# Reciprocal denominators broadcast as bf16 in 16 transfers a half, scaled on ScalarE and multiplied on VectorE; the sixth product ahead of the second in the down stage

## The chip, the cores and the metric

The kernel runs on one core of one Trainium2 chip. The core has TensorE (PE, matmuls into PSUM), VectorE (DVE), ScalarE (ACT), GpSimd (POOL) and SyncE (SP, which here only issues DMA transfers). Each engine works through its own list of instructions in order and waits on semaphores for the others; 16 DMA engines move data between memory and SBUF. The metric is the device time of one launch in microseconds (us), the median of several runs.

## What is computed

The input `x` has 2048 tokens of 1024 features. Layer norm, then linear attention with 32 heads of 32, then a gated feed-forward of width 3584 on the same normalised input, whose output gates the attention's:

```python
phi = lambda t: jnp.where(t > 0, t + 1, jnp.exp(t)) + 1e-6
pq, pk = phi(q), phi(k)
kv = jnp.einsum("bhsd,bhse->bhde", pk, v)
z = jnp.einsum("bhsd->bhd", pk)
num = jnp.einsum("bhqd,bhde->bhqe", pq, kv)
den = jnp.einsum("bhqd,bhd->bhq", pq, z)[..., None] + 1e-6
o = num / den
...
xn = _layernorm(x, axis=-1)
s = _A_ref(xn, A_wqkv, A_wo)                      # o @ wo
g = silu((silu(xn @ w_gate) * (xn @ w_up)) @ w_down)
return x + s * g
```

Inputs, weights and output are bf16. The place that the change touches is the division by `den`, one number for each token and head.

## The kernel before

**Stages.** The first 140 us or so normalise `x`, transpose it (fp16, features on the partitions, in the arenas X and P), project keys and values and sum up `kv` and `z` over all tokens. Then `kv`, divided by `z` and masked to the diagonal blocks of the heads, is multiplied with `wo` into one 1024 x 1024 matrix M: 16 single matmuls, `m_build(g, c)`, each copied by ACT out of PSUM and stored to `m_scratch` in memory. With M, attention's second part is one product: s = (phi(q) z / den) @ M.

After that two halves of 1024 tokens (`p` = 0, 1) follow, each in the same order: the pairs q0, g0, q1, g1, g2 ... g13, then four down blocks. A pair holds two products of 1024 tokens by 1024 by 256 columns, each through a seven-product scheme (class `Set`, steps numbered 1 to 7) that takes seven multiplications of half-size blocks in place of eight; a pair has 56 matmuls of 128 x 512. The scheme needs sums and differences of weight blocks (`wload`, DVE), of activation blocks, and of results in PSUM: step 1 copies a bank on ACT, step 5 is copied to SBUF by ACT, steps 6 and 7 add on DVE. The results of steps 2, 3, 4 and 7 are final and go on to an evacuation by ACT or DVE. `PAIRSEQ` is the order in which a pair's steps stand.

- A q pair computes q and phi(q) into a bf16 tile in the arena H (`pq_tile`, 52 to 68 KB), and collects `den` on TensorE.
- A g pair (`gu_pair`) computes gate and up for 256 of the 3584 columns and writes silu(gate) * up to H.
- A down block `c` (`d_set`) covers 256 output columns: one product D of the gated values with `w_down` and one product S of the divided phi(q) with M. Their steps stand in the string `seq`. Step 6 adds step 5's copy to a bank on DVE, into another bank; step 7 then goes on in the old bank, so D7 waits for D6's addition. Step 4 of D needs seven differences R10 - T2, made by DVE just ahead into a ring of two buffers (`t4_ring`).

**Division, before.** Both halves call `recip(p)` and `normalise(p)` behind pair g1. `recip` takes the reciprocals of `den` on DVE (L769, L772) and stores them in fp32 to `r_scratch` in memory, 128 KB. `normalise` goes over 16 tiles (two token blocks `j` by eight head groups `g`). For each tile four transfers bring the reciprocals of four heads, each row repeated over 32 partitions, into a slot of `rr_ring`, a ring of three; ACT scales the slot by `z` (L308); POOL multiplies phi(q) with it (L791), and a transfer of 128 KB stores the result to `q_scratch`. So that is 64 broadcasts and 16 stores a half. `pq_load` reads `q_scratch` back before the down blocks, into X, as the operand of S.

**What sets the order.** Nothing runs as it is written: every operation is recorded in a `Plan` with what it reads and writes, and a list scheduler with its own cost figures (for a transfer 0.08 us of SP plus its bytes in a serial queue) puts each engine's operations into a fixed order. Within an engine nothing overtakes. All transfers are issued by SP, in one order, and a transfer that waits for a buffer holds up the ones behind it. Matmuls are recorded by the helper at L195, transposes by that at L202, ACT's work at L308, DVE's two-input operations at L315, transfers at L318. Weights come through `wload`: raw weights in a ring of three places, their sums in another ring of three. The names in the profile: `ps` is a PSUM bank, `W` the weight arena, `TM` the arena of temporaries, `H`, `X` and `P` as above, `zc` holds `z`.

Of the kernel before, what the change touches and what calls it, by code (L numbers as in the profile page):

```python
# [205 lines left out]
def build_kernel(nc, A_x, A_wqkv, A_wo, B_w_gate, B_w_up, B_w_down, out, WINDOW=6, NWARM=14):  # L206
# [12 lines left out]
    with ExitStack() as es:  # L219
# [20 lines left out]
        def named(*key):  # L240
            return Region([key])
# [23 lines left out]
        r_scr = nc.dram_tensor("r_scratch", [2, 4, 32, 256], F32)  # L265
# [54 lines left out]
        class Ring:  # L320
# [3 lines left out]
            def take(self):  # L324
                k = self.k % self.n
                self.k += 1
                return Slot(self.a, self.off + k * self.size, self.size, k)

# [277 lines left out]
        class Set:  # L606
# [4 lines left out]
            def __init__(self, ops, evac):  # L611
                self.ops, self.evac = ops, evac
# [15 lines left out]
            def step(self, m):  # L628
# [19 lines left out]
                elif m == 7:  # L648
                    self.grp(7, self.b, False)
                    d = d_ring.take()  # L650
# [13 lines left out]
        class Places(Ring):  # L664
            def __init__(self, arena, offs, size):
                self.a, self.offs, self.size, self.k = arena, offs, size, 0

            def take(self):
                k = self.k % len(self.offs)
                self.k += 1  # L670
                return Slot(self.a, self.offs[k], self.size, k)

        raw_ring = Places(W, (0, 8 * KB, 16 * KB), 8 * KB)
        cmb_ring = Places(W, (44 * KB, 24 * KB, 32 * KB), 8 * KB)
# [24 lines left out]
        def xset(stat, w, xv, evac):  # L699
            def ops(m):  # L700
                ws, wr = stat(w, m)
                xa, xr = xv[XOF[m]]
                return 4, [([(ws[q], xa[:, q, :]) for q in range(4)], [wr, xr])]
            return Set(ops, evac)
# [32 lines left out]
        def pq_tile(g, j):  # L737
            o = PQ0 + (2 * g + j) * KB
            return H.at(o, KB, BF16), H.reg(o, KB)

        def q_pair(p, s, stat, at=()):
# [18 lines left out]
            run_pair(xset(stat, 0, XV[p], evac(0)), xset(stat, 1, XV[p], evac(1)), at)  # L760

        def recip(p):
# [4 lines left out]
            ea, ra = e.ap(F32, 0, KB), e.ap(F32, KB, KB)  # L767
# [6 lines left out]
            dma([rr], [named("rscr", p)], r_scr[p].rearrange("q h t -> (q h) t"), ra, dsem("rs"), 128 * KB)  # L774

        def normalise(p):

            for j in range(2):
                for g in range(NG):
                    src, sr = pq_tile(g, j)  # L780
                    dst = src.bitcast(FP16)
                    e = rr_ring.take()
                    first = None
                    for hl in range(4):
                        rows = r_scr[p, 2 * j:2 * j + 2, 4 * g + hl, :].partition_broadcast(32)
                        o0 = dma([named("rscr", p)], [e.r],
                                 TM.t[32 * hl:32 * hl + 32, e.off // 2:(e.off + e.size) // 2].bitcast(F32).rearrange(
                                     "p (q t) -> p q t", q=2), rows, dsem("rr%d_%d" % (e.k, hl)), 64 * KB, first)
                        first = first or o0
                    act([z_r, e.r], [e.r], e.ap(F32), e.ap(F32), ACT.Identity, "sb", scale=zc[:, g:g + 1])  # L790
                    pool([sr, e.r], [sr], lambda h, dst=dst, src=src, e=e: h.tensor_tensor(  # L791
                        dst, src, e.ap(F32), ALU.mult), 1.35)
                    dma([sr], [named("q", p, g, j)], q_scr[p, g // 4, j, :, (g % 4) * 512:(g % 4 + 1) * 512], dst,
                        dsem("pq%d" % (g % 4)), 128 * KB)
# [17 lines left out]
        def gu_pair(p, n, stat):  # L812
# [11 lines left out]
            run_pair(xset(stat, 0, XV[p], ev_g), xset(stat, 1, XV[p], ev_u))  # L824
# [7 lines left out]
        def pq_load(p):  # L832
            for j in range(2):
                for k in range(2):
                    v, vr = xblock(X, 2 * j + k)
                    dma([named("q", p, 4 * k + g, j) for g in range(4)], [vr], v, q_scr[p, k, j].rearrange(
# [5 lines left out]
        t4_ring = Ring(W, 40 * KB, 2 * KB, 2)  # L842
# [51 lines left out]
        def d_set(p, c, Sx, mstat, first):  # L894
# [61 lines left out]
            dset = Set(dops, keep(gv, ACT.Silu))  # L956
            sset = xset(mstat, 0, QV, keep(sv, ACT.Identity))
# [123 lines left out]
```

## Time and profile before

| | us |
|---|---|
| median of three runs | 814.59 (814.16 to 815.94) |
| the profiled execution's own time | 815.25 |
| its span | 813.5 |

Between the profiled execution's time and its span lie 1.75 us outside the profile. A table of stages, from the windows of the profile (busy microseconds of each engine in the stretch):

| from : to | what | length | PE | DVE | ACT | POOL | granted clock |
|---|---|---|---|---|---|---|---|
| 0 : 140 | layer norm, keys, values | 140.0 | 133.8 | 75.6 | 56.8 | 11.5 | 1.00 |
| 140 : 208 | q0, g0, q1, g1, M | 68.0 | 66.9 | 50.7 | 38.7 | 4.4 | 1.00 |
| 208 : 262 | pairs with the division, first half | 54.0 | 42.4 | 27.1 | 23.5 | 16.7 | 0.91 |
| 262 : 360 | the rest of the g pairs | 98.0 | 98.0 | 69.2 | 37.5 | 0.0 | 1.00 |
| 360 : 480 | down blocks, first half | 120.0 | 116.9 | 73.8 | 28.9 | 0.0 | 1.00 |
| 480 : 542 | q0, g0, q1, g1 | 62.0 | 61.8 | 46.0 | 33.1 | 3.8 | 1.00 |
| 542 : 588 | pairs with the division, second half | 46.0 | 37.4 | 32.2 | 21.2 | 17.5 | 0.96 |
| 588 : 690 | the rest of the g pairs | 102.0 | 100.1 | 72.9 | 38.7 | 0.0 | 1.00 |
| 690 : 813 | down blocks, second half | 123.0 | 115.9 | 64.6 | 28.1 | 0.0 | 1.00 |

How to read it: an engine loses nothing by being idle unless another waits for it, so the column of TensorE against the length shows where time goes, and the views of waits show for whom it waited. In a row of a view, `[2.32 <-ACT ps L308]` is the idle time just before the instruction and the work that ended last before it began. A row like "x28 | 17.8, 289 | 47.0 <-ACT ..." gives the count, the busy time and mean in ns of one, and the idle time before the group.

### The profile page before, as it was taken

The page shows a single profiled execution, that of the slowest core. Times are in us where ns is not written, and L with a number is a line of the kernel's source. Part 1 is how long each engine was busy: PE and PEld are TensorE (multiplying, and loading weights), DVE is VectorE, ACT ScalarE, POOL GpSimd, SP SyncE. Part 2 cuts the span into 40 slices and gives each one's busy share as a digit, 9 for nine tenths or more (in the row PEclk, how much of TensorE's full clock was granted, in tenths as well). Part 3 has the DMA queues.
Part 4 walks back from the last instruction along what each step waited for, and adds up shares of the span by engine and source line. Part 5 has one row for each costly group of instructions (what it writes and reads, how often), then busy time and mean ns, then how long its engine had stood idle before and what let it go on. Part 6 is the DMA issues. An engine that isn't in the chain of part 4 may idle for free.

```text
span 813.5 us, 9849 instructions
## 1 busy us (share of the span) xinstructions
PE 773.1 (95%) x3800; PEld 349.5 (43%) x3818; DVE 512.1 (63%) x913; ACT 306.4 (38%) x505; POOL 53.9 (7%) x65
## 2 busy tenths in 40 slices
PE   8999999999778999999999999988899999999997
PEld 3445554444323444444444444333344444444443
DVE  5587434767365668686464776786767767657353
ACT  3344443565443343422322234545443333232131
POOL 2020000000341000000000000034200000000000
PEclk9999999999998999999999999999999999999999
DMA  9921000135665332551623522257852341351510
GB/s 307 261 66 39 1 1 1 52 111 140 181 189 151 104 104 54 140 173 47 195 77 92 146 74 84 73 161 210 257 142 65 92 135 34 91 160 48 155 39 27
DMA packets 147888, 91.10 MB, mean 112 GB/s; under 512 B 5248, under 2 KB 144768, under 8 KB 147840
## 3 DMA queue, kind: packets, MB, share of 16 engines
q1 hardware_dynamic: 147840, 90.46, 39.1%
q8 instruction: 30, 0.49, 0.3%
q14 instruction: 18, 0.15, 0.1%
HBM read 79.69 MB, written 10.75 MB: 111 GB/s over the span
## 4 chain that ended last, share of the span: by engine, by line
PE 69%; DMA 11%; SPq 8%; DVE 6%; ACT 2%; issue 2%; POOL 1%; DVEq 0%
PE ps L195 68%; SPq L318 8%; DVE W L315 3%; DMA W<-m_scratch 3%; DMA W<-in_B_w_up_dram 2%; DMA TM<-r_scratch 2%; PE ps L202 1%; DMA H<-in_A_wqkv_dram 1%; DMA W<-in_B_w_down_dram 1%; DVE TM L315 1%; ACT TM L308 1%; POOL H L791 1%; DVE ps L315 1%; DMA W<-in_A_wqkv_dram 1%; DMA m_scratch<-H 0%
## 5 line engine op out<-in xcount | busy, mean ns | idle before, releaser
L195 PE MATMUL ps<-X,W 128*128 128x512 f16 x1504 | 354.9, 385 | 21.7 <-DVE ps L315 12.9
L308 ACT ACTIVATE TM<-ps 128x512 f32<-128x512 f32 (+2 forms) x300 | 176.3, 595 | 274.7 <-PE ps L195 274.3
L195 PEld LDWEIGHTS ps<-X,W 128*128 128x128 f16 (+1 forms) x1504 | 144.5, 99 | 203.0 <-DVE ps L315 17.8
L315 DVE TENSOR_TENSOR W<-W 128x1024 f16<-128x1024 bf16 (+3 forms) x224 | 143.1, 654 | 80.5 <-DMA W<-in_B_w_up_dram 36.5
L195 PE MATMUL ps<-H,W 128*128 128x512 f16 x672 | 150.7, 379 | 2.5 <-DVE ps L315 2.2
L195 PE MATMUL ps<-P,W 128*128 128x512 f16 x512 | 123.4, 380 | 1.3 <-ACT ps L308 1.3
L315 DVE TENSOR_TENSOR ps<-ps,TM 128x512 f32<-128x512 f32 x80 | 55.6, 694 | 76.4 <-PE ps L195 76.3
L195 PEld LDWEIGHTS ps<-H,W 128*128 128x128 f16 (+1 forms) x672 | 64.9, 98 | 80.4 <-DVE ps L315 3.2
L315 DVE TENSOR_TENSOR TM<-ps,TM 128x512 f32<-128x512 f32 (+1 forms) x112 | 67.7, 606 | 48.4 <-PE ps L195 44.4
L308 ACT ACTIVATE ps<-ps 128x512 f32<-128x512 f32 x80 | 46.7, 584 | 96.7 <-PE ps L195 96.4
L195 PEld LDWEIGHTS ps<-P,W 128*128 128x128 f16 (+1 forms) x512 | 49.2, 98 | 60.4 <-ACT ps L308 1.8
L791 POOL TENSOR_TENSOR H<-H,TM 128x512 f16<-128x512 bf16 x32 | 42.3, 1332 | 459.1 <-ACT TM L308 459.1
L308 ACT ACTIVATE TM<-TM 128x512 f16<-128x512 f32 x52 | 32.6, 626 | 78.2 <-DVE TM L315 78.1
L315 DVE TENSOR_TENSOR H<-ps,TM 128x512 f16<-128x512 f32 x84 | 57.0, 685 | 6.7 <-PE ps L195 5.4
L195 PE MATMUL ps<-H,X 128*128 128x512 bf16 x249 | 56.4, 379 | 3.0 <-ACT X L308 2.0
L195 PE MATMUL ps<-H,P 128*128 128x512 bf16 x248 | 56.1, 379 | 0.4
L485 DVE TENSOR_SCALAR TM<-TM 128x512 f16<-128x512 f16 x64 | 17.8, 289 | 47.0 <-ACT TM L308 46.3
L315 DVE TENSOR_TENSOR W<-H 128x1024 f16<-128x1024 f16 x56 | 38.2, 701 | 1.1 <-PE ps L195 0.3
L308 ACT ACTIVATE TM<-TM,zc 128x512 f32<-128x512 f32 x32 | 23.0, 720 | 39.8 <-DMA TM<-r_scratch 39.8
L195 PEld LDWEIGHTS ps<-H,X 128*128 128x128 f16 x256 | 24.4, 98 | 30.9 <-ACT X L308 2.1
L195 PEld LDWEIGHTS ps<-H,P 128*128 128x128 f16 x256 | 24.8, 98 | 28.3
L195 PE MATMUL ps<-W 128*128 128x512 f16 x112 | 31.2, 380 | 2.2 <-DVE W L315 1.9
(60 smaller groups left out, 317.9 us busy)
## 6 DMA issues: line engine op xcount, KB each, us to landing
W<-in_B_w_gate_dram SPq DMA_DIRECT2D x28, 512.0 KB, 4.1
W<-in_B_w_up_dram SPq DMA_DIRECT2D x28, 512.0 KB, 5.4
W<-in_B_w_down_dram SPq DMA_DIRECT2D x16, 896.0 KB, 6.9
TM<-r_scratch SPq DMA_DIRECT2D x128, 64.0 KB, 2.7
W<-in_A_x_dram SPq DMA_DIRECT2D x16, 256.0 KB, 3.3
H<-in_A_wqkv_dram SPq DMA_DIRECT2D x4, 1024.0 KB, 9.0
W<-in_A_wqkv_dram SPq DMA_DIRECT2D x8, 512.0 KB, 7.5
q_scratch<-H SPq DMA_DIRECT2D x32, 128.0 KB, 2.7
```

The lines of the kernel that those rows point to most:

```text
L195: last = h.matmul(o, l, r, start=st, stop=sp, skip_group_check=True)
L202: last = h.transpose(o, i, ident)
L308: return PL.op("act", reads, writes, lambda h: h.activation(o, i, func, **kw), nel(o) / 1200.0 + (0.055 if src == "ps" else 0.095))
L315: return dve(reads, writes, lambda h: h.tensor_tensor(o, a, b, op), nel(o), 1.92 if fast else 0.96)
L318: return PL.op("sp", reads, writes, lambda h: h.dma_start(o, i), 0.08, sem=s, nbytes=nbytes, cow=cow)
L485: dve([e.r], [b.r], lambda h: h.tensor_scalar(ba, ea, 1.0, EPS_PHI, ALU.min, ALU.add), 512, 2.6)
L791: pool([sr, e.r], [sr], lambda h, dst=dst, src=src, e=e: h.tensor_tensor(dst, src, e.ap(F32), ALU.mult), 1.35)
```

## The change

*Denominators.* `r_scratch` is bf16: `recip` gets one more ACT operation that writes the reciprocals as bf16, and the store has 64 KB. `normalise` first sends 16 broadcasts, eight for each token block `j` (four head positions by two token quarters); each fills 32 partitions with eight head groups of 256 tokens. They go to 16 KB of H of their own, 68 to 84 KB, which hold `wo` until the last `m_build` of the first half; so the `m_build` products come in groups of 8 and 8 behind g0 and g1 (before: 6, 6 and 4 behind g0, g1 and g2). Every ACT scaling of a block `j` depends on all eight of its transfers. ACT scales in bf16 in place, DVE multiplies (before POOL), and four stores of 512 KB replace 16 of 128 KB, with `pq_tile` laid out to suit.

*Down blocks.* `seq` has D6 ahead of D2. `t4_ring` gets a third buffer, the last of three of `d_ring`; the down blocks keep to the other two (`dd_ring`).

```diff
-        r_scr = nc.dram_tensor("r_scratch", [2, 4, 32, 256], F32)
+        r_scr = nc.dram_tensor("r_scratch", [2, 4, 32, 256], BF16)
...
         def pq_tile(g, j):
-            o = PQ0 + (2 * g + j) * KB
+            o = PQ0 + ((2 * (g // 4) + j) * 4 + g % 4) * KB
...
-            dma([rr], [named("rscr", p)], r_scr[p].rearrange("q h t -> (q h) t"), ra, dsem("rs"), 128 * KB)
+            act([rr], [er], rb, ra, ACT.Identity, "sb")
+            dma([er], [named("rscr", p)], r_scr[p].rearrange("q h t -> (q h) t"), rb, dsem("rs"), 64 * KB)
+
+        RB0 = 68 * KB
 
         def normalise(p):
 
             for j in range(2):
+                rb = H.at(RB0 + j * 8 * KB, 8 * KB).rearrange("p (g q t) -> p g q t", g=NG, q=2)
+                rbr = H.reg(RB0 + j * 8 * KB, 8 * KB)
+                first = None
+                for hl in range(4):
+                    rows = r_scr[p, 2 * j:2 * j + 2, :, :].rearrange("q (g h) t -> h g q t", h=4)[hl]
+                    for q in range(2):
+                        o0 = dma([named("rscr", p)], [rbr], rb[32 * hl:32 * hl + 32, :, q, :],
+                                 rows[:, q, :].partition_broadcast(32), dsem("rr%d_%d_%d" % (j, hl, q)), 128 * KB, first)
+                        first = first or o0
                 for g in range(NG):
                     src, sr = pq_tile(g, j)
                     dst = src.bitcast(FP16)
-                    e = rr_ring.take()
-                    first = None
-                    for hl in range(4):
-                        rows = r_scr[p, 2 * j:2 * j + 2, 4 * g + hl, :].partition_broadcast(32)
-                        o0 = dma([named("rscr", p)], [e.r],
-                                 TM.t[32 * hl:32 * hl + 32, e.off // 2:(e.off + e.size) // 2].bitcast(F32).rearrange(
-                                     "p (q t) -> p q t", q=2), rows, dsem("rr%d_%d" % (e.k, hl)), 64 * KB, first)
-                        first = first or o0
-                    act([z_r, e.r], [e.r], e.ap(F32), e.ap(F32), ACT.Identity, "sb", scale=zc[:, g:g + 1])
-                    pool([sr, e.r], [sr], lambda h, dst=dst, src=src, e=e: h.tensor_tensor(
-                        dst, src, e.ap(F32), ALU.mult), 1.35)
-                    dma([sr], [named("q", p, g, j)], q_scr[p, g // 4, j, :, (g % 4) * 512:(g % 4 + 1) * 512], dst,
-                        dsem("pq%d" % (g % 4)), 128 * KB)
+                    o = RB0 + j * 8 * KB + g * KB
+                    zr, zrr = H.at(o, KB), H.reg(o, KB)
+                    act([z_r, zrr], [zrr], zr, zr, ACT.Identity, "sb", scale=zc[:, g:g + 1])
+                    tt([sr, zrr], [sr], dst, src, zr, ALU.mult, True)
+            for j in range(2):
+                for k in range(2):
+                    o = PQ0 + (2 * k + j) * 4 * KB
+                    dma([H.reg(o, 4 * KB)], [named("q", p, k, j)], q_scr[p, k, j], H.at(o, 4 * KB, FP16),
+                        dsem("pq%d%d" % (k, j)), 512 * KB)
...
-        t4_ring = Ring(W, 40 * KB, 2 * KB, 2)
+        t4_ring = Places([(W, 40 * KB), (W, 42 * KB), (TM, 8 * KB)], 2 * KB)
+        dd_ring = Ring(TM, 4 * KB, 2 * KB, 2)
...
             if first:
-                seq = "D1 D5 D2 D6 D7 S1 S5 D3 S2 S6 D4 S7 S3 S4"
+                seq = "D1 D5 D6 D2 D7 S1 S5 D3 S2 S6 D4 S7 S3 S4"
             else:
-                seq = "S1 S5 S2 S6 D1 S7 S3 D5 S4 D2 D6 D7 D3 D4"
+                seq = "S1 S5 S2 S6 D1 S7 S3 D5 S4 D6 D2 D7 D3 D4"
...
-                if p == 0 and n < 3 and k == "g":
-                    for _ in range(6):
+                if p == 0 and n < 2 and k == "g":
+                    for _ in range(8):
                         if mb:
                             m_build(*mb.popleft())
```

`Places` is a ring whose buffers stand at listed places; `first` lets the transfers into one buffer go side by side.

**SP, the first half behind pair g1, before.** A row gives the line, the operation, destination and source, the size, and how many stand in a row.

```order
L318 DMA TM<-r_scratch 32x2x256 x12
L318 DMA m_scratch<-H 128x512 x3
L318 DMA TM<-r_scratch 32x2x256 x4
L318 DMA q_scratch<-H 128x512
L318 DMA m_scratch<-H 128x512
L318 DMA TM<-r_scratch 32x2x256 x4
L318 DMA q_scratch<-H 128x512
L318 DMA m_scratch<-H 128x512
L318 DMA TM<-r_scratch 32x2x256 x4
L318 DMA q_scratch<-H 128x512
L318 DMA W<-in_B_w_gate_dram 128x8x256
L318 DMA W<-in_B_w_up_dram 128x8x256
```

The same place of the change:

```order
L318 DMA m_scratch<-H 128x512 x4
L318 DMA r_scratch<-TM 128x256
L318 DMA m_scratch<-H 128x512 x2
L318 DMA H<-r_scratch 32x8x256 x16
L318 DMA TM<-in_A_x_dram 128x4x256
L318 DMA m_scratch<-H 128x512 x2
L318 DMA W<-in_B_w_gate_dram 128x8x256
L318 DMA W<-in_B_w_up_dram 128x8x256
L318 DMA q_scratch<-H 128x2048 x3
L318 DMA W<-in_B_w_gate_dram 128x8x256
L318 DMA W<-in_B_w_up_dram 128x8x256
L318 DMA q_scratch<-H 128x2048
```

All 16 broadcasts now stand in one run, the weight loads behind them rather than among them, and the four stores between weight loads.

**ACT, the first half, in the pairs behind g1, before.** `TM<-TM,zc` is a scaling by `z`, `ps<-ps` the copy of step 1, `TM<-ps` the copies and silus, `H<-ps` the copies of `m_build`.

```order
L308 ACTIVATE TM<-TM,zc 128x512
L308 ACTIVATE H<-ps 128x512 x2
L308 ACTIVATE TM<-TM,zc 128x512
L308 ACTIVATE H<-ps 128x512
L308 ACTIVATE ps<-ps 128x512
L308 ACTIVATE TM<-TM,zc 128x512
L308 ACTIVATE H<-ps 128x512
L308 ACTIVATE ps<-ps 128x512
L308 ACTIVATE TM<-ps 128x512 x3
L308 ACTIVATE TM<-TM,zc 128x512
L308 ACTIVATE TM<-ps 128x512
L308 ACTIVATE TM<-TM,zc 128x512
```

And of the change, where a scaling reads `H<-H,zc`:

```order
L308 ACTIVATE ps<-ps 128x512
L308 ACTIVATE H<-H,zc 128x512
L308 ACTIVATE TM<-ps 128x512
L308 ACTIVATE H<-H,zc 128x512
L308 ACTIVATE ps<-ps 128x512
L308 ACTIVATE H<-H,zc 128x512
L308 ACTIVATE TM<-ps 128x512 x2
L308 ACTIVATE H<-H,zc 128x512 x8
L308 ACTIVATE TM<-ps 128x512
L308 ACTIVATE H<-H,zc 128x512 x2
L308 ACTIVATE TM<-ps 128x512
L308 ACTIVATE H<-H,zc 128x512 x3
```

The scalings, before spread over several pairs, stand close together, eight of them in one run.

**TensorE, a down block behind the first one (c = 2 of the first half), before.** `ps<-X,W` are matmuls of S, `ps<-H,W` and `ps<-W` of D, `ident,TM` the transposes of a finished tile. The four `ps<-X,W` are S4.

```order
L195 MATMUL ps<-X,W 128x512 x8
L195 MATMUL ps<-H,W 128x512 x7
L195 MATMUL ps<-X,W 128x512 x4
L195 MATMUL ps<-H,W 128x512 x35
L202 MATMUL ps<-ident,TM 128x128 x4
L195 MATMUL ps<-H,W 128x512 x28
L195 MATMUL ps<-W 128x512 x4
```

And of the change:

```order
L195 MATMUL ps<-X,W 128x512 x8
L195 MATMUL ps<-H,W 128x512 x7
L195 MATMUL ps<-X,W 128x512 x4
L195 MATMUL ps<-H,W 128x512 x42
L202 MATMUL ps<-ident,TM 128x128 x4
L195 MATMUL ps<-H,W 128x512 x14
L195 MATMUL ps<-TM,W 128x512 x2
L195 MATMUL ps<-H,W 128x512 x7
```

Steps 2, 3, 5, 6 and 7 of D are 14 matmuls each. Before, the 35 behind S4 are the second half of D5, then D2, then D6; the 28 are D7 and D3. Now the 42 are the second half of D5, D6, D2 and the first half of D7, so D2's 14 stand between D6 and D7, and the first of D4's operands here comes from the new buffer in TM.

40 lines of the change are left out of this document (20 added, 20 removed).

## The prediction

> **What bounds the kernel now.** First I read the page's head: TensorE is the bound, and what it loses sits in a few slices.
>
> ```profile
> PE 773.1 (95%) x3800; PEld 349.5 (43%) x3818; DVE 512.1 (63%) x913; ACT 306.4 (38%) x505; POOL 53.9 (7%) x65
> PE   8999999999778999999999999988899999999997
> PEclk9999999999998999999999999999999999999999
> ```
>
> Slices 11 to 13 and 29 to 31 (20.3 us each) read 7 and 8; they lie where each half divides phi(q) by its denominators. Windows cut there, beside a clean stretch and the two down stages, read:
>
> ```profile
> 262.10:360.00 97.90, 97.90 (x454) 44.29 (x453) 69.18 (x109) 37.45 (x64) 0.00 (x0) 1.00 0.38 105
> 380.00:477.00 97.00, 93.89 (x467) 42.54 (x466) 57.83 (x108) 24.33 (x42) 0.00 (x0) 1.00 0.42 117
> 710.00:811.00 101.00, 95.87 (x478) 42.89 (x475) 52.35 (x104) 24.70 (x43) 0.00 (x0) 1.00 0.30 84
> 207.90:262.10 54.20, 42.60 (x168) 16.66 (x168) 27.20 (x40) 23.51 (x41) 16.68 (x13) 0.91 0.64 188
> 542.30:588.20 45.90, 37.10 (x161) 15.66 (x159) 32.44 (x41) 21.16 (x36) 17.54 (x13) 0.96 0.77 221
> ```
>
> The columns are start:end and length, busy time of PE, PEld, DVE, ACT, POOL, then the granted clock, DMA share and GB/s. The clean stretch never idles. Its pace: 93 matmuls between these two starts take 20.09 us, 0.216 us each, so one weight pair (56 matmuls) takes 12.1 us.
>
> ```profile
> 339.83 20.25 PE L195 MATMUL ps<-X,W 128*128 128x512 f16 x93
> 359.92 2.32 PE L195 MATMUL ps<-H,W 128*128 128x512 f16 x10
> ```
>
> Window 207.9 holds 167 matmuls (timeline count; the window says 168): 36.1 us of work, so **18.1 us are lost**. Window 542.3 holds 160: 34.6 us, **11.3 us lost**. Part is waiting, part a slower clock behind the waits:
>
> ```profile
> 214.41 7.90 PE L195 MATMUL ps<-X,W 128*128 128x512 f16 x28 [2.32 <-ACT ps L308]
> 232.34 6.22 PE L195 MATMUL ps<-X,W 128*128 128x512 f16 x28 [1.72 <-ACT ps L308]
> 241.62 14.16 PE L195 MATMUL ps<-X,W 128*128 128x512 f16 x56 [3.07 <-DVE ps L315]
> 257.73 1.04 PE L195 MATMUL ps<-X,W 128*128 128x512 f16 x4 [1.94 <-DVE ps L315]
> ...
> 559.31 3.38 PE L195 MATMUL ps<-X,W 128*128 128x512 f16 x8 [2.99 <-DVE ps L315]
> ```
>
> The same 28 matmuls take 7.90 us behind a wait of 2.32 us and 6.22 behind 1.72. Who makes ACT and DVE late? The waits in 190 to 262 and SP's timeline say:
>
> ```profile
> ACT TM L308 <- DMA TM<-r_scratch: 26.4, 16, 5.2
> DVE W L315 <- DMA W<-in_B_w_up_dram: 10.7, 4, 3.6
> ...
> 233.32 4.41 SPq L318 DMA_DIRECT2D TM<-r_scratch  x4
> 243.03 3.06 SPq L318 DMA_DIRECT2D TM<-r_scratch  x4
> 249.46 0.80 SPq L318 DMA_DIRECT2D W<-in_B_w_up_dram  x1
> ```
>
> SP works through 64 broadcasts and 16 stores one by one, each waiting for a buffer that ACT and POOL must free (ring of three). Weight loads queue behind; DVE stands at their arrival with TensorE's additions behind it, and ACT at each broadcast with TensorE's copies behind it.
>
> **The change part by part.**
>
> ```profile
> L791 POOL TENSOR_TENSOR H<-H,TM 128x512 f16<-128x512 bf16 x32 | 42.3, 1332 | 459.1 <-ACT TM L308 459.1
> L308 ACT ACTIVATE TM<-TM,zc 128x512 f32<-128x512 f32 x32 | 23.0, 720 | 39.8 <-DMA TM<-r_scratch 39.8
> L315 DVE TENSOR_TENSOR TM<-TM 128x512 f16<-128x512 f16 x32 | 13.5, 420 | 13.2 <-ACT TM L308 13.2
> L485 DVE TENSOR_SCALAR TM<-TM 128x512 f16<-128x512 f16 x64 | 17.8, 289 | 47.0 <-ACT TM L308 46.3
> W<-in_B_w_up_dram SPq DMA_DIRECT2D x28, 512.0 KB, 5.4
> TM<-r_scratch SPq DMA_DIRECT2D x128, 64.0 KB, 2.7
> q_scratch<-H SPq DMA_DIRECT2D x32, 128.0 KB, 2.7
> ```
>
> *Queue.* Per half, 64 broadcasts and 16 stores become 16 and 4. At 0.47 us an issue (12 in 5.50 us in a row below) that is 37.6 us of SP against 9.4. All 16 broadcasts now have their own place, so none waits for ACT. Weights for pair 5 stand behind the 16, pair 6 behind three stores.
>
> ```profile
> 192.08 0.34 SPq L318 DMA_DIRECT2D r_scratch<-TM  x1
> ...
> 529.59 1.81 DMA r_scratch<-TM
> ...
> 531.41 5.50 SPq L318 DMA_DIRECT2D TM<-r_scratch  x12
> ```
>
> *When the first half's burst lands.* Pair 2 ends on TensorE at 207.9 now; four `m_build` matmuls move ahead of it (0.9 us) and, below, cost 1 us: 209.8. The new bf16 copy stands on ACT behind three evacuations of pair 2, done about 202.4, so the store leaves ten microseconds later than its 192.08, with nothing on TensorE waiting. It lands 1.8 later (529.59 to 531.41 in the chain), and 16 issues run from 204.4 to 212. An eighth is 128 KB in 256 pieces; eight are 1 MB in 512-byte pieces, just like a gate and up load, whose second lands 5.4 us after its issue. So the first eight are down at about 211, between 208.2 + 1.7 and 208.2 + 7.3 (least and most of the old broadcasts, row below).
>
> ```profile
> DMA to landing us min/median/max: 1.7/2.7/7.3
> ```
>
> *ScalarE.* 16 scalings in both versions; bf16 is not in the trace, so 0.60 to 0.72 us, the PSUM-source and fp32 rows; I take 0.62 start to start. In the first half all 16 stand between pair 3's first copy and pair 4's: 9.9 us beside pair 3's own eight evacuations of 0.5, 13.9 us of work in a 12.1 us pair. Pair 4's first copy thus comes at 225.7, where TensorE's fourth step wants it at 224.5. With some slip of the landing I charge **2.0**. In the second half four scalings stand in pair 2's tail, twelve in pair 3 (11.4 in 12.1): **1.0**. Ends: 0 and 7 for each, the upper if the burst lands 4 us later and the clock drops too.
>
> *VectorE* takes over the multiplication: 16 per half at 0.42 (bounds 0.29, a one-input op, and 0.69, fp32), 6.7 us across pairs 2 to 4, where the clean window leaves it idle 28.7 of 97.9, 3.5 us a pair. POOL's 1.33 us operations go; no one else used it. Three multiplications stand ahead of pair 3's first PSUM addition: scaled by 214.5, while that addition is due at 215.0. Cost zero, with 0.8 us of cover; past it, one for one.
>
> *The `m_build` products*, 8 + 8 instead of 6 + 6 + 4. Each needs an evacuation:
>
> ```profile
> L308 ACT ACTIVATE H<-ps 128x512 f16<-128x512 f32 x16 | 8.7, 601 | 2.3 <-PE ps L195 2.3
> 174.20 1.90 PE L195 MATMUL ps<-X,W 128*128 128x512 f16 x8 [0.67 <-DVE ps L315]
> ```
>
> Two more lengthen the ACT chain behind that 0.67 us wait by about 1.0 while TensorE gains 0.43 of work; the same after pair 1. Charge **1.0** (0 to 2).
>
> *Down stage.* D6 now stands ahead of D2, so 14 matmuls (3.0 us) cover the addition that D7 waits for; a third place serves the 701 ns subtractions of D4.
>
> ```profile
> 435.14 1.56 DVE L315 TENSOR_TENSOR W<-W 128x512 f16<-128x512 f16 x4 [1.03 <-DMA W<-m_scratch]
> ...
> 437.70 6.22 PE L195 MATMUL ps<-H,W 128*128 128x512 f16 x28 [0.21 <-DVE ps L315]
> 445.32 0.60 PE L195 MATMUL ps<-W 128*128 128x512 f16 x2 [0.21 <-DVE W L315]
> 467.02 6.22 PE L195 MATMUL ps<-H,W 128*128 128x512 f16 x28 [0.57 <-DVE ps L315]
> 474.87 0.61 PE L195 MATMUL ps<-W 128*128 128x512 f16 x2 [0.78 <-DVE W L315]
> ...
> 675.56 1.04 PE L195 MATMUL ps<-X,W 128*128 128x512 f16 x4 [1.69 <-DVE TM L315]
> ...
> 797.60 6.22 PE L195 MATMUL ps<-H,W 128*128 128x512 f16 x28 [0.57 <-DVE ps L315]
> ```
>
> Block 3 waits for nothing else (0.57, twice): gone. Blocks 1 and 2 have the addition behind the arrival of m_scratch, issued when S4 ends in both versions, so it is late again; about half stays. I take 2.0 from D6 and 0.5 from D4, **2.5** together; bounds 0 and 5, about the idle of the two down windows (3.1 and 5.1) without the tail. A late down-weight load (1.69 us of idle at 675) is untouched.
>
> [...] The trace lost clock behind waits of 1.94 to 3.07 us: 0.91 and 0.96 granted in the two stages, 1.00 elsewhere. [...]
>
> **Rivals.**
> 1. *The wait only moves.* ACT and DVE serve in order, and their first scaling waits for eight transfers at once. For: one microsecond of slack; 13.9 us of ACT work in a 12.1 us pair. Against: the 5.4 us landing. Price if the eight land at the old 7.3 us: 4 more a half plus 1.5 of clock, 11 in all: 798.
> 2. *The clock loss isn't the waits'.* Of 29.4 us lost, waits in the timeline make 20.3; 9.1 are clock. If that stays: 796. Against: 6.22 beside 7.90 above.
> 3. *It doesn't relieve the DMA.* As many pieces move as before (16 x 256 = 64 x 64), and the share there was 0.64 and 0.77. If pieces, not issues, held up the weights, half the gain goes: 801. Against: the share is short of full, and SP's stops come with full rings.
> 4. *Slower.* The eight broadcasts read the same 4 KB again and again; if that serialises them, the first scaling stops ACT, copies and TensorE one for one. It decides once the landing takes 18 us rather than 3 (14 us a half cancel the 28 gained); at 25 us the time is 829. The old broadcasts never took over 7.3.
>
> **How the numbers follow.** 18.1 + 11.3 - 2.0 - 1.0 - 1.0 + 2.5 = 27.9 us off the profiled run (span 813.5, run 815.25, so 1.75 around it): 787.4. The median of three is 814.59, 0.66 lower: **787**. Chances: forecast (781 to 793) 0.68, rival 1 (793 to 804) 0.17, rival 2 0.05, rival 3 0.06, slower 0.04. Everything going well, with no charges and 5 from the down stage, gives 780; the upper end takes in rivals 1 and 2: 780 to 799. 0.2% (1.6 us) is about what a measurement here can tell from no change: faster 0.95, same 0.01, slower 0.04.
>
> **What would show it.** Right: TensorE at nearly 10 of 10 in pairs 2 to 6 of both halves, clock 1.00 there; 32 broadcasts, issued at about 0.47; no DVE wait for up weights there; POOL empty after the start; DVE some 13 us busier; no wait of 0.57 at block 3's D7. Wrong: waits of over 2 us by TensorE for ACT's copies at pairs 3 and 4 (rival 1), a clock under 1.00 without waits (2), weights landing later than 6 us (3), broadcasts landing after ten or more (4).

## The result, and the profile after

The changed kernel takes 789.71 us (789.6 to 791.02, three runs) against 814.59: 0.9696 of the time before (95% interval 0.9672 to 0.9719). The profiled execution took 789.71 with a span of 787.9, so 25.6 us of span are gone; the prediction had 27.9 gone and a time of 787. The page's head and TensorE's slices:

```profile
PE 763.0 (97%) x3818; PEld 347.7 (44%) x3818; DVE 513.2 (65%) x945; ACT 305.0 (39%) x507; POOL 11.5 (1%) x33
...
PE   8999999999999999999999999999999999999997
...
PEclk9999999999999999999999999999999999999999
```

The 7s and 8s of slices 11 to 13 and 29 to 31 are gone, the granted clock reads 9 in every slice (0.999 over the run), and POOL is down to the work at the start. Where in the program did the time go? Four landmarks of TensorE's timeline cut every kernel here in the same way: the first matmul behind keys and values, the first matmul of D in the first half, the first den matmul of the second half, the first matmul of D there. For the kernel before the first two are at 140.74 and 359.92, and the others are (start, length, instruction):

```profile
486.86 0.29 PE L195 MATMUL ps<-H,Zh 128*32 128x256 bf16 x2
...
690.24 12.25 PE L195 MATMUL ps<-H,W 128*128 128x512 f16 x56
```

For the changed kernel:

```profile
140.40 0.40 PE L195 MATMUL ps<-ones,ident 128*128 128x128 f16 x4 [0.29 <-DVE H L585]
...
345.54 13.93 PE L195 MATMUL ps<-H,W 128*128 128x512 f16 x63
...
470.33 0.29 PE L195 MATMUL ps<-H,Zh 128*32 128x256 bf16 x2
...
665.51 12.25 PE L195 MATMUL ps<-H,W 128*128 128x512 f16 x56
```

| us | before | after | gain | prediction |
|---|---|---|---|---|
| A: to D of the first half (first division) | 219.18 | 205.14 | 14.0 | 18.1 - 2.0 - 1.0 = 15.1 |
| B: down blocks and what runs beside them, first half | 126.94 | 124.79 | 2.2 | B and D: 2.5 |
| C: to D of the second half (second division) | 203.38 | 195.18 | 8.2 | 11.3 - 1.0 = 10.3 |
| D: down blocks, second half, to the end | 123.26 | 122.39 | 0.9 | |

The rest, 0.3 us, is ahead of the first landmark. What TensorE still waits for in the two divisions stands in its timeline:

```profile
215.74 3.63 PE L195 MATMUL ps<-X,W 128*128 128x512 f16 x16 [1.55 <-ACT ps L308]
219.96 6.28 PE L195 MATMUL ps<-X,W 128*128 128x512 f16 x28 [0.59 <-DVE ps L315]
227.25 118.45 PE L195 MATMUL ps<-X,W 128*128 128x512 f16 x548 [1.02 <-ACT ps L308]
...
531.88 1.90 PE L195 MATMUL ps<-P,W 128*128 128x512 f16 x8 [1.51 <-ACT ps L308]
...
554.01 1.04 PE L195 MATMUL ps<-X,W 128*128 128x512 f16 x4 [1.12 <-DVE TM L315]
```

Three waits of 3.16 us in the first half and two of 2.63 in the second, in place of the rows of 1.72 to 3.07 before. 28 matmuls behind the second wait take 6.28, near the 6.22 of the kernel before behind 1.72 us and not the 7.90 behind 2.32. SP's timeline and ACT's show how the burst runs:

```profile
201.69 2.27 SPq L318 DMA_DIRECT2D r_scratch<-TM  x1
...
205.61 7.88 SPq L318 DMA_DIRECT2D H<-r_scratch  x16
```

```profile
213.38 0.72 ACT L308 ACTIVATE H<-H,zc 128x512 bf16<-128x512 bf16 x1 [2.89 <-DMA H<-r_scratch]
...
215.10 0.58 ACT L308 ACTIVATE ps<-ps 128x512 f32<-128x512 f32 x1
...
217.18 5.00 ACT L308 ACTIVATE H<-H,zc 128x512 bf16<-128x512 bf16 x8
```

Sixteen issues at 0.49 us each, never stopped. ACT comes free at 210.5, stands 2.89 us at the landing of the first eight, and only then gets to pair 3's copies; the one at 215.10 ends TensorE's wait of 1.55. From 217.18 eight scalings run at 0.62 us from start to start.

### The profile page after: what moved, and what is told of

It is laid out like the page before. It is cut to its first block, busy times and chain, and to the rows that moved or that the text cites. A ratio compares the mean times of both kernels' runs of the same rounds, so it can differ in the third digit from the quotient of the medians.

```text
span 787.9 us, 9684 instructions
## 1 busy us (share of the span) xinstructions
PE 763.0 (97%) x3818; PEld 347.7 (44%) x3818; DVE 513.2 (65%) x945; ACT 305.0 (39%) x507; POOL 11.5 (1%) x33
## 4 chain that ended last, share of the span: by engine, by line
PE 81%; DMA 10%; ACT 4%; DVE 3%; SPq 2%; issue 1%; ACTq 0%
PE ps L195 79%; DMA W<-m_scratch 4%; ACT H L308 2%; PE ps L202 2%; SPq L318 2%; DMA H<-in_A_wqkv_dram 1%; DMA W<-in_B_w_down_dram 1%; DMA H<-r_scratch 1%; DVE W L315 1%; DMA W<-in_B_w_up_dram 1%; ACT TM L308 1%; DVE ps L315 1%; DMA m_scratch<-H 0%; DVE TM L315 0%; ACT ps L308 0%
## 5 line engine op out<-in xcount | busy, mean ns | idle before, releaser
L195 PE MATMUL ps<-X,W 128*128 128x512 f16 x1504 | 346.7, 379 | 7.7 <-DVE TM L315 2.8
L315 DVE TENSOR_TENSOR W<-W 128x1024 f16<-128x1024 bf16 (+3 forms) x224 | 137.3, 629 | 73.2 <-DMA W<-in_B_w_down_dram 34.3
L195 PE MATMUL ps<-H,W 128*128 128x512 f16 x672 | 153.3, 379 | 4.2 <-DVE ps L315 4.0
L308 ACT ACTIVATE TM<-TM 128x512 f16<-128x512 f32 (+1 forms) x54 | 33.5, 620 | 56.6 <-DVE TM L315 56.4
L315 DVE TENSOR_TENSOR H<-H 128x1024 f16<-128x1024 f16 (+1 forms) x74 | 41.6, 571 | 12.2 <-ACT H L308 11.2
L315 DVE TENSOR_TENSOR W<-H 128x1024 f16<-128x1024 f16 x38 | 25.4, 685 | 0.5
L308 ACT ACTIVATE H<-H,zc 128x512 bf16<-128x512 bf16 x32 | 20.8, 716 | 5.0 <-DMA H<-r_scratch 5.0
L495 DVE SCALAR_TENSOR_TENSOR W<-ps,TM 128x512 bf16<-128x512 f32 x32 | 22.0, 688 | 0.8
```

The costliest lines, as they stand in the source:

```text
L195: last = h.matmul(o, l, r, start=st, stop=sp, skip_group_check=True)
L308: return PL.op("act", reads, writes, lambda h: h.activation(o, i, func, **kw), nel(o) / 1200.0 + (0.055 if src == "ps" else 0.095))
L315: return dve(reads, writes, lambda h: h.tensor_tensor(o, a, b, op), nel(o), 1.92 if fast else 0.96)
L495: dve([src_r, b.r], [out_r], lambda h: h.scalar_tensor_tensor(out_ap, src, 0.0, ba, ALU.max, ALU.add), 512)
```

## The experiments

Each edit is to the changed kernel unless it says otherwise. The kernels before and after ran again beside them on other chips, where the kernel before took 816 to 817 us, so times are compared as ratios to it and the stages by the landmarks above. The division's code is the same in five profiles (the changed kernel twice and the three of the down blocks): A and C together are 399.2 to 400.5 us there, so a difference of 1.3 there is within the spread of single profiles.

| us | A | B | C | D | A + C | B + D | ratio to before (95%) |
|---|---|---|---|---|---|---|---|
| before | 219.18 | 126.94 | 203.38 | 123.26 | 422.6 | 250.2 | 1 |
| changed | 205.14 | 124.79 | 195.18 | 122.39 | 400.3 | 247.2 | 0.9696 (0.9672 to 0.9719) |
| after_again | 205.41 | 124.97 | 194.41 | 121.94 | 399.8 | 246.9 | 0.9676 (0.9646 to 0.9705) |
| e4_pool_mult | 214.05 | 124.37 | 197.30 | 121.03 | 411.4 | 245.4 | 0.9767 (0.9727 to 0.9808) |
| e5_before_dve_mult | 216.80 | 128.40 | 204.89 | 124.38 | 421.7 | 252.8 | 0.9989 (0.9966 to 1.0012) |
| e6_64_transfers | 223.66 | 125.73 | 217.17 | 123.67 | 440.8 | 249.4 | 1.0191 (1.0151 to 1.0231) |
| e7_first_eight_twice | 207.30 | 124.51 | 197.81 | 121.80 | 405.1 | 246.3 | 0.9734 (0.9710 to 0.9758) |
| e8_no_scaling | 208.24 | 123.39 | 195.39 | 122.22 | 403.6 | 245.6 | 0.9705 (0.9670 to 0.9740) |
| e10_no_scaling_late | 201.89 | 123.34 | 191.80 | 121.75 | 393.7 | 245.1 | 0.9571 (0.9542 to 0.9600) |
| e13_scaling_late | 202.33 | 124.01 | 192.37 | 121.70 | 394.7 | 245.7 | 0.9585 (0.9559 to 0.9611) |
| e12_both | 201.51 | 122.50 | 190.26 | 119.02 | 391.8 | 241.5 | 0.9502 (0.9467 to 0.9538) |
| e1_division_only | 204.91 | 128.09 | 195.38 | 123.52 | 400.3 | 251.6 | 0.9706 (0.9670 to 0.9742) |
| e2_d6_only | 205.39 | 127.27 | 195.07 | 123.52 | 400.5 | 250.8 | 0.9696 (0.9666 to 0.9725) |
| e3_t4_only | 204.96 | 126.55 | 194.21 | 122.34 | 399.2 | 248.9 | 0.9681 (0.9658 to 0.9705) |

### Is it the transfers or the multiplication that moved?

The multiplications back on POOL:

```diff
-                    tt([sr, zrr], [sr], dst, src, zr, ALU.mult, True)
+                    pool([sr, zrr], [sr], lambda h, dst=dst, src=src, zr=zr: h.tensor_tensor(
+                        dst, src, zr, ALU.mult), 1.35)
```

> The changed kernel with the multiplications back on POOL (1.33 us each, 21 us a half). Theory (the queue on SP and the waits tile by tile were what was lost): nothing on TensorE waits for the products before the down blocks, so only VectorE's slower operations beside POOL cost something, 0 to 3 us: 790 to 793. Rival (the slow multiplication on POOL held the old ring, and moving it is the gain): half or more of the 25 us comes back, 802 or more.

Neither: the span is 797.0, 9.1 over the changed kernel, and A and C take 11.0 more. TensorE has one long wait:

```profile
237.03 102.36 PE L195 MATMUL ps<-X,W 128*128 128x512 f16 x460 [5.78 <-DVE ps L315]
```

VectorE is late there because its own operations are slow: from 223.28 it works without a pause up to the addition that ends this wait. Its groups by form in 213 to 236, the stretch in which POOL multiplies almost without a pause, first for this kernel:

```profile
L315 DVE TENSOR_TENSOR H<-H 128x1024 f16<-128x1024 f16 x3 | 4.6, 1520 | 0.1
L315 DVE TENSOR_TENSOR W<-W 128x1024 f16<-128x1024 bf16 x3 | 4.5, 1538 | 2.9 <-DMA W<-in_B_w_up_dram 2.8
L315 DVE TENSOR_TENSOR H<-ps,TM 128x512 f16<-128x512 f32 x3 | 2.0, 683 | 1.5 <-ACT TM L308 1.5
```

and for the changed kernel:

```profile
L315 DVE TENSOR_TENSOR H<-ps,TM 128x512 f16<-128x512 f32 x4 | 2.7, 684 | 0.0
L315 DVE TENSOR_TENSOR W<-W 128x1024 f16<-128x1024 bf16 x4 | 2.7, 684 | 0.0
L315 DVE TENSOR_TENSOR H<-H 128x1024 f16<-128x1024 f16 x3 | 2.1, 684 | 0.0
```

Beside POOL these two-input operations with both operands in SBUF take 1520 and 1538 ns instead of 684; the three forms with an operand in PSUM stay at 683, 690 and 700 (684, 686 and 693 in the changed kernel). With two more of 1036 and 1037 ns, eight operations take 5.8 us more than without POOL, as long as TensorE's wait. The two sources differ only in where the multiplication runs, so POOL's work is what slows them. Moving the multiplication thus frees VectorE; the sum had POOL's operations as used by no one else, and counted nothing for it.

The move alone, made to the kernel before:

```diff
-                    pool([sr, e.r], [sr], lambda h, dst=dst, src=src, e=e: h.tensor_tensor(
-                        dst, src, e.ap(F32), ALU.mult), 1.35)
+                    tt([sr, e.r], [sr], dst, src, e.ap(F32), ALU.mult)
```

> The kernel before with one edit: VectorE multiplies (fp32 by bf16, about 0.69 us) in place of POOL; 64 broadcasts and 16 stores a half and the ring of three stay. Theory of the queue: SP still issues 80 transfers one by one and stops at the ring; at most a third of the gain, 806 to 815, or slower than before if VectorE now stands at ACT's scalings. Rival (POOL's 1.33 us sets when a slot of the ring is free): two thirds of the gain or more, 798 or less.

Nothing is gained (0.9989, interval across 1). The waits in 190 to 262 (us in total, times, longest) are those of before with VectorE in POOL's place:

```profile
ACT TM L308 <- DMA TM<-r_scratch: 23.5, 15, 5.8
...
DVE H L315 <- ACT TM L308: 9.4, 10, 2.4
DVE W L315 <- DMA W<-in_B_w_up_dram: 8.6, 4, 2.6
```

So POOL's 1.33 us did not hold the ring: ACT waits for the broadcasts nearly as long (23.5 us, before 26.4), and VectorE now stands 9.4 us at ACT's scalings. The multiplication's place is worth nothing with the old transfers and 11 us with the new ones.

### The number of transfers

The same bytes and the same pieces in 64 transfers, with a place for each tile:

```diff
-                for hl in range(4):
-                    rows = r_scr[p, 2 * j:2 * j + 2, :, :].rearrange("q (g h) t -> h g q t", h=4)[hl]
-                    for q in range(2):
-                        o0 = dma([named("rscr", p)], [rbr], rb[32 * hl:32 * hl + 32, :, q, :],
...
+                for g in range(NG):
+                    first = None
+                    for hl in range(4):
+                        rows = r_scr[p, 2 * j:2 * j + 2, 4 * g + hl, :].partition_broadcast(32)
+                        o0 = dma([named("rscr", p)], [H.reg(RB0 + j * 8 * KB + g * KB, KB)],
+                                 rb[32 * hl:32 * hl + 32, g, :, :], rows, dsem("rr%d_%d_%d" % (j, g, hl)), 32 * KB, first)
+                        first = first or o0
```

> The changed kernel with the broadcasts cut as before into 64 a half (four for each tile, 32 KB), each tile's scaling waiting for its own four, but with a place for every tile, so no ring. The bytes and the number of 512-byte pieces are those of the changed kernel; SP issues for 30 us rather than 8, with the weights of pairs 5 and 6 behind them. Theory (the issue count on the one queue is what was lost, as the prediction's term for the queue has it): the weights come late and VectorE stands at them, half or more of the gain goes, 800 to 808. Rival (it was the ring of three and the stops at it; issues alone are cheap): 788 to 794.

Worse than the theory, and slower than the kernel before: A and C take 440.8, 40 us more than with 16 transfers and 18 more than with the ring. SP issues for 30 us without a stop, a tile's four take 1.9 us, and ACT stands at every tile with TensorE's copy behind it; first SP, then ACT, then TensorE:

```profile
206.83 30.33 SPq L318 DMA_DIRECT2D H<-r_scratch  x64
238.14 0.50 SPq L318 DMA_DIRECT2D W<-in_B_w_gate_dram  x1
```

```profile
214.24 0.72 ACT L308 ACTIVATE H<-H,zc 128x512 bf16<-128x512 bf16 x1 [1.17 <-DMA H<-r_scratch]
216.19 0.72 ACT L308 ACTIVATE H<-H,zc 128x512 bf16<-128x512 bf16 x1 [1.23 <-DMA H<-r_scratch]
218.31 0.72 ACT L308 ACTIVATE H<-H,zc 128x512 bf16<-128x512 bf16 x1 [1.39 <-DMA H<-r_scratch]
218.93 0.58 ACT L308 ACTIVATE ps<-ps 128x512 f32<-128x512 f32 x1
```

```profile
219.57 8.34 PE L195 MATMUL ps<-X,W 128*128 128x512 f16 x28 [6.30 <-ACT ps L308]
```

The price is the count of issues on the one queue, not the bytes, the pieces or the ring, in the order that this scheduler makes. It reckons 0.08 us of SP for an issue, against 0.47 here, and in SP's order of the kernel before the next pair's weights stood behind 24 broadcasts, here behind all 64. What 64 issues would cost in an order made with their true price was not run, nor were the four stores in place of 16 tried alone.

### What still waits: the landing, or ACT's work

The first eight broadcasts of a half twice, and the first block's scalings behind both (the copy goes to a free place in H, `dv`, region `du`):

```diff
+                    for hl in range(4):
+                        rows = r_scr[p, 2 * j:2 * j + 2, :, :].rearrange("q (g h) t -> h g q t", h=4)[hl]
+                        for q in range(2):
+                            o0 = dma([named("rscr", p)], [du], dv[32 * hl:32 * hl + 32, :, q, :],
...
-                    act([z_r, zrr], [zrr], zr, zr, ACT.Identity, "sb", scale=zc[:, g:g + 1])
+                    act([z_r, zrr] + ([du] if j == 0 else []), [zrr], zr, zr, ACT.Identity, "sb", scale=zc[:, g:g + 1])
```

> The changed kernel with the first eight broadcasts of each half sent a second time, to a free place in H, and the scalings of the first block made to wait for these too: the first scaling can start about 3.8 us later (eight more issues at 0.47 us). Theory (ACT stands at the landing and TensorE's copies behind it one for one, as the first rival of the prediction has it; TensorE waited 1.55 us in the first half and 1.51 in the second): 3 to 4 us more a half, 6 to 8 us over the changed kernel, 796 to 798. Rival (there is cover of 2 us or more a half behind the landing): 0 to 3 us over it, 790 to 793.

Between the two: A and C are 4.8 to 5.3 us over the changed kernel's two profiles, 2.5 a half. But the run is no clean measure of the cover. The first scaling came 13.4 and 13.2 us after the burst's first issue, not 3.8 but 5.6 and 5.8 later than in the changed kernel, and the scheduler, which knew of the added transfers, put ACT's copies ahead of it. TensorE's long waits moved to VectorE, whose additions stand behind multiplications that wait for the scalings:

```profile
223.16 126.28 PE L195 MATMUL ps<-X,W 128*128 128x512 f16 x576 [3.94 <-DVE ps L315]
...
541.03 1.58 PE L195 MATMUL ps<-X,W 128*128 128x512 f16 x4 [2.85 <-DVE ps L315]
```

So a later landing does cost TensorE time; how much of it the changed kernel's own order covers stays open.

The scalings taken out; `kv` is divided by `ZS` (2048) in place of `z`, and the reciprocals come out 2048 times as large:

```diff
-                    KVZ[:, g, :], kvp[:, 0:128], zinv[:, g:g + 1], maskbd[:, :], ALU.mult, ALU.mult), 128)
+                    KVZ[:, g, :], kvp[:, 0:128], 1.0 / ZS, maskbd[:, :], ALU.mult, ALU.mult), 128)
...
-            dve([bank_r[db]], [er], lambda h: h.tensor_scalar(ea, ps[db][:, 0:256], 16.0, EPS_PHI, ALU.mult, ALU.add), 256)
+            dve([bank_r[db]], [er], lambda h: h.tensor_scalar(ea, ps[db][:, 0:256], 16.0 / ZS, EPS_PHI / ZS, ALU.mult, ALU.add), 256)
...
-                    act([z_r, zrr], [zrr], zr, zr, ACT.Identity, "sb", scale=zc[:, g:g + 1])
```

> The changed kernel without ACT's 32 scalings: kv is divided by 2048 instead of z, and the reciprocals are multiplied by 2048 in the operation that adds the epsilon, so the quotient is the same and VectorE multiplies the broadcast itself. Theory (the burst of scalings on ACT costs TensorE 1.55 + 0.59 + 1.02 us in the first half and 1.51 in the second): the waits for ACT's copies at these places go, 785 to 787. Rival (TensorE waits for the landing of the broadcasts, and VectorE will stand at it in ACT's place, up to eleven multiplications in a row ahead of its additions): 789 to 793.

The rival holds: A and C take 403.6, 3.5 more than with scalings. VectorE stands where ACT stood, and TensorE's addition behind it:

```profile
214.58 2.77 DVE L315 TENSOR_TENSOR H<-H 128x512 f16<-128x512 bf16 x8 [3.88 <-DMA H<-r_scratch]
219.83 1.10 DVE L315 TENSOR_TENSOR H<-H 128x512 f16<-128x512 bf16 x3 [2.48 <-DMA H<-r_scratch]
220.84 0.69 DVE L315 TENSOR_TENSOR ps<-ps,TM 128x512 f32<-128x512 f32 x1
```

The first issue was at 206.50: the first eight are down 8.0 us later, the second eight 13.3. The scheduler reckoned with 5.6 and 9.1 and so put eleven multiplications ahead of that addition. The next kernel corrects that figure and nothing else; the number in `dma` only enters the model, which then puts every engine's order anew:

```diff
-                                 rows[:, q, :].partition_broadcast(32), dsem("rr%d_%d_%d" % (j, hl, q)), 128 * KB, first)
+                                 rows[:, q, :].partition_broadcast(32), dsem("rr%d_%d_%d" % (j, hl, q)), 224 * KB, first)
```

> Without scalings as before this, and with the broadcasts entered in the scheduler's model with 224 KB each in place of 128 (no byte more is moved): in the profile the first eight were down 8.0 us after their first issue and the second eight 13.3, the model had 5.6 and 9.1. So VectorE's order has the multiplications behind the landing. Theory (VectorE stood at the landing with TensorE's additions behind it: 4.71 and 3.54 us): these waits fall under 1.5 us together, the two stages outside the down blocks take 395 to 398 us in place of 403.6, the whole about 5 us under the changed kernel. Rival (the wait is for VectorE's own time, 16 more operations): 401 to 404, no gain.

A and C fall to 393.7, ten below the run before, and TensorE no longer waits in the two stretches (windows 207.9 to 235 and 523 to 560; PE busy is the whole length):

```profile
207.90:235.00 27.10, 27.10 (x127) 12.09 (x126) 23.06 (x45) 10.17 (x18) 0.00 (x0) 1.00 0.96 249
523.00:560.00 37.00, 37.00 (x173) 16.80 (x172) 29.80 (x55) 14.00 (x24) 0.00 (x0) 1.00 0.80 233
```

Now the same line alone, with the scalings kept:

> The changed kernel with its scalings, and only the broadcasts entered in the scheduler's model with 224 KB in place of 128. It tells the two halves of what TensorE still waited for apart: ACT standing at the landing, which the model's order should take away, and ACT's own time for 16 scalings, which stays. The two stages outside the down blocks took 400.1 us in the changed kernel (mean of two) and 393.7 without scalings and with this order. Theory (the landing is most of it): 394 to 396.5. Rival (the scalings' own 9.9 us on ACT, 13.9 us of work in a pair of 12.1, as the prediction's term has it): 398 to 400.5.

394.7 is what the theory said. With ACT's order right, 16 scalings a half cost at most the 1.0 us to the run without them, which is within the spread; two waits of 0.47 and 0.44 us for ACT's copies are left. So 5.4 us of what the changed kernel still pays is a matter of order. Its timeline puts 4.7 us of waiting (3.16 and 1.51) at ACT and VectorE behind the landing, engines that serve in order and meet a transfer too early. The other wait, 1.12 us for up weights in the second half, goes too, because SP's new order has these weights ahead of the loads of X. ACT's rows now, and the wait that is left in the first half:

```profile
213.29 0.60 ACT L308 ACTIVATE TM<-ps 128x512 f16<-128x512 f32 x1 [0.28 <-PE ps L195]
213.78 0.71 ACT L308 ACTIVATE H<-H,zc 128x512 bf16<-128x512 bf16 x1
...
224.95 118.73 PE L195 MATMUL ps<-X,W 128*128 128x512 f16 x548 [0.47 <-ACT ps L308]
```

ACT's first copies of pair 3 now stand ahead of the first scaling, which waits for nothing.

### The down blocks

Three kernels, each undoing a part: both (e1), the third buffer only (e2), the order only (e3).

```diff
-                seq = "D1 D5 D6 D2 D7 S1 S5 D3 S2 S6 D4 S7 S3 S4"
+                seq = "D1 D5 D2 D6 D7 S1 S5 D3 S2 S6 D4 S7 S3 S4"
...
-        t4_ring = Places([(W, 40 * KB), (W, 42 * KB), (TM, 8 * KB)], 2 * KB)
+        t4_ring = Ring(W, 40 * KB, 2 * KB, 2)
```

> The new division with the down blocks as before (D2 ahead of D6, a ring of two for D4's differences). Theory: the two stages of the division give 22.2 of the 25.6 us by which the two spans differ, the down blocks 3.0 (measured from landmark to landmark), so about 792.7 us, 3.0 over the changed kernel. Rival: the down blocks differ only by when their weights happen to land, and the order is worth nothing: 789.7 +- 0.8.

> The changed kernel with the old ring of two for D4's differences; D6 stays ahead of D2. Both down stages together (from the first matmul of D to the first den matmul of the second half, and from the first of D there to the end) took 250.2 us before, 247.2 in the changed kernel, 251.6 with the old order and the old ring. Theory (D6's order is most of it, as in the sum: 2.0 against 0.5): 247 to 249. Rival (the third buffer is what counts; D7 still waits 0.3 to 1.4 us, so the order gives little): 250 to 252.

> The changed kernel with D2 ahead of D6 as before; the ring of three for D4's differences stays. Down stages together: theory (D6's order is most of it) 250 to 251.5; rival (the third buffer is it) 247 to 248.5. The span of the rest as in the changed kernel within 0.7 us.

The changed kernel itself ran with them:

> The changed kernel once more, beside the three others on one chip: 0.9696 of the time before, within 0.3%; both theories expect the same.

B and D together: with neither edit 250.2, 251.6 and 252.8 (before, e1, e5), with both 245.1 to 249.4 in eight profiles, mean 246.5. So the two are worth about 5 us, not 2.5 or the 3.0 read from one pair of profiles. The third buffer alone gives 248.9, within the spread of the kernels with both; the order alone gives 250.8, within that of the kernels with neither. Single profiles thus speak against the sizes of the sum (2.0 for the order, 0.5 for the buffer), but don't settle the shares: the profiled execution of e2 was the slowest of its four (793.78 us, median 791.53), and the whole times can't tell these kernels apart, as their intervals overlap.

Nor does the gain lie where the sum put it. Of the 3.0 us by which B and D are shorter, 0.2 is idle time of TensorE (11.0 us before, 10.8 after); its busy time for the same matmuls is 2.8 shorter, and why is open. Its waits for D4's differences fell from 1.9 us to none, but those of D's matmuls for an addition of VectorE grew: 2.2 us before, 2.7 in e1, 6.7 with the order alone, 2.0 with the buffer alone, 4.0 with both.

Why the order gave little: D7 still waits, in the changed kernel 1.25 us at 394.96 in block 1, though 14 matmuls now stand ahead of it. VectorE's rows there, then those ahead of block 2's D7, which waits 0.26 us:

```profile
391.31 2.98 DVE L315 TENSOR_TENSOR W<-W 128x896 f16<-128x896 bf16 x6 [7.67 <-DMA W<-in_B_w_down_dram]
394.21 0.69 DVE L315 TENSOR_TENSOR ps<-ps,TM 128x512 f32<-128x512 f32 x1
...
421.26 1.56 DVE L315 TENSOR_TENSOR W<-W 128x512 f16<-128x512 f16 x4 [1.01 <-DMA W<-m_scratch]
422.74 0.69 DVE L315 TENSOR_TENSOR ps<-ps,TM 128x512 f32<-128x512 f32 x1
```

D6's addition is the second row of each pair. In block 1 it stands behind six sums of `w_down`, which came late, later than the scheduler had it; in block 2 behind sums that wait for `m_scratch`. The last kernel corrects the figure for `w_down` too, on top of e10:

```diff
-                dma([], [r], v, wd_v[:, k, :, c * 256:(c + 1) * 256], dsem("dg%d" % (o // (8 * KB))), 896 * KB)
+                dma([], [r], v, wd_v[:, k, :, c * 256:(c + 1) * 256], dsem("dg%d" % (o // (8 * KB))), 1408 * KB)
```

> The one before, and the loads of w_down entered in the model with 1408 KB in place of 896 (again no byte more): in the profile they land 7.1 us after their issue. Theory (D6's addition stands on VectorE behind weight sums that wait for w_down's landing, and that is what D7 still waits for, 1.2 to 1.6 us at three blocks, and the 1.2 to 1.7 us at the end of the last pair): down blocks 243 to 245 us in place of 247, and 1 us less ahead of them; some 8 us under the changed kernel, 781 to 783. Rival (w_down itself arrives too late, and the order can't help): within 1 us of the one before.

B and D 241.5, the whole 775.4 us (775.23 to 777.11) and 0.9502 of the time before: better than expected, and the best kernel here. Two sums instead of six precede the addition, and it then waits for TensorE:

```profile
384.00 1.28 DVE L315 TENSOR_TENSOR W<-W 128x896 f16<-128x896 bf16 x2 [4.56 <-DMA W<-in_B_w_down_dram]
388.03 0.70 DVE L315 TENSOR_TENSOR ps<-ps,TM 128x512 f32<-128x512 f32 x1 [2.75 <-PE ps L195]
```

The correction moved SP's order as well (a `w_down` load ahead of the loads of `x`), so the share of each is open. No wait of D's matmuls for an addition is left in this profile.

## Why the prediction was right, and where it was off

**The bound and its cause** were right: SP's queue. Two experiments bracket it, 64 issues without a ring (440.8 in A and C) and the multiplication moved without the transfers (421.7, before 422.6). The burst came at 0.49 us an issue, charged were 0.47. What was missing is that the gain needs both parts: with the transfers alone (multiplication on POOL) A and C give 11.2 us of the 22.2.

**The clock** came back with the waits: 1.00 in both stages. The second rival falls, the third too: a DMA share of 0.95 and 0.96 was no bound in these stretches, since in the first of them e10's TensorE never waits at 0.96. The changed kernel's windows:

```profile
207.90:235.00 27.10, 23.94 (x110) 10.19 (x108) 19.92 (x39) 17.72 (x32) 0.00 (x0) 1.00 0.95 247
523.00:560.00 37.00, 34.37 (x159) 14.91 (x157) 27.71 (x52) 23.12 (x40) 0.00 (x0) 1.00 0.96 261
```

**The landing** was the step that failed. The store of the reciprocals was given 1.8 us, from the profile of before; it took 3.3 (median of two issues). The burst began at 205.6, not 204.4, its first eight took 7.8 us from the first issue, not 6.6, and were down at 213.4, not "about 211". The ACT term of 2.0 and 1.0 was mis-sized (3.16 with 0.59 for VectorE, and 1.51), and its reason was mostly wrong: 13.9 us of ACT work in a pair of 12.1 costs about 1 us (e13 against e10), ACT standing at the landing with copies behind it costs most of the rest. That is the first rival's mechanism; it came true in the small, some 4 us against its 11.

**VectorE:** 16 multiplications at 0.42 us, as taken. They were not quite free: the addition that TensorE awaits for 0.59 us stands behind two of them, which had waited for scalings. "Some 13 us busier" was wrong: 513.2 against 512.1. The multiplications added 12.8, and the groups of two-input operations with both operands in SBUF took some 10 us less, as they no longer run beside POOL.

**`m_build`:** 1.0 was charged; the wait at its first bunch went from 0.67 to 0.90 us.

**Not in the sum:** 1.12 us at 554.01 for up weights of the second half. They were issued at 543.95, among the loads of X from `q_scratch`, and VectorE stood 2.04 us for them.

**The down blocks:** right in sign and near in size, but by luck, since the term's mechanism failed. That "14 matmuls (3.0 us) cover the addition that D7 waits for" holds only where nothing holds up VectorE ahead of that addition. Block 3 no longer waits at D7, as forecast. Block 2 still waits behind the arrival of `m_scratch`, as forecast, 0.26 us in the first half and 1.15 in the second. But block 1 of the first half waits behind sums of `w_down`, 1.25, and so does block 0 of the second, 1.38, which the sum didn't have. Together the waits at D7 grew from 2.2 to 4.0 us, and TensorE's gain there came as shorter busy time, with its cause open.

**The slower rival** did not come: eight broadcasts, each reading 4 KB of its own 32 times, are down 7.8 us after their first issue (8.0 in e8) and about 4 after their last, far from the 18 at which it would decide.

## What to carry to other kernels

Where one queue issues everything, count the issues between two loads that matter: 64 of them cost 18 us more than the ring that throttled them, and the same bytes in 16 cost 40 us less than in 64. Behind a burst, look at which in-order engine meets its landing first and what stands behind that instruction; telling the scheduler the landing that the profile shows was worth 5.4 us here, and as much again for the weights, with no work changed. Two edits can be worth nothing and 11 us alone, and 22 together, so try each on the kernel before and undo each in the kernel after.

## What the runs showed of the hardware

VectorE's two-input operations of 128x1024 with both operands in SBUF took 1520 and 1538 ns on average beside a busy POOL (e4; two single ones 1036 and, with 128x512 from fp32, 1037) and 682 to 685 without it; those that read PSUM took 683 to 700 beside POOL and 684 to 693 without.

In these traces the granted clock did not follow from the length of a wait alone. Behind 2.32 us of waiting the kernel before got 0.50 of its clock (windows below; PE's busy time, then the clock after POOL's), and 0.55 in 259 to 261, behind 1.94 us at 257.73. Behind 3.54 us at 540.79 the kernel without scalings (e8) kept it: 1.00 in each window of 2 us from 540 to 546. What it did follow from, no run here shows.

```profile
212.00:214.00 2.00, 0.10 (x1) 0.00 (x0) 0.00 (x0) 1.33 (x3) 0.54 (x1) 1.00 0.52 164
216.00:218.00 2.00, 2.00 (x6) 0.73 (x5) 0.00 (x0) 1.93 (x4) 1.13 (x1) 0.50 0.65 144
```

```profile
540.00:542.00 2.00, 1.21 (x6) 0.60 (x7) 2.00 (x6) 0.00 (x0) 0.00 (x0) 1.00 1.08 398
542.00:544.00 2.00, 2.00 (x11) 0.74 (x9) 2.00 (x4) 0.78 (x2) 0.00 (x0) 1.00 1.03 422
544.00:546.00 2.00, 2.00 (x11) 0.94 (x10) 2.00 (x4) 0.93 (x2) 0.00 (x0) 1.00 1.04 391
```

```profile
540.79 1.04 PE L195 MATMUL ps<-X,W 128*128 128x512 f16 x4 [3.54 <-DVE ps L315]
```
